# 64x64 state tiles, w_in loaded by blocks of 128 rows, and a new order in a fused attention and MLP kernel

## The chip, the cores and the metric

The kernel runs on one core of a Trainium2 chip. The metric is the device time of one execution in microseconds, median of several runs. A run more than 1.5% above the fastest of its kernel counts as slow, and only fast runs enter a ratio. A time is the median of all runs of a kernel; the difference between two kernels is that of the means of their fast runs. The core's parts are called as in the profile: PE is TensorE, DVE is VectorE, ACT is ScalarE, POOL is GpSimd, SP is SyncE.

## The reference

Linear attention with decay (4 batches, 8 heads, 768 positions, 64 channels), then a two-layer MLP with ELU on the 3072 tokens. Cut to what matters:

```python
for b in range(nb):                      # blocks of positions
    intra = einsum('bhic,bhjc->bhij', qb, kb) * Dmask
    intra = einsum('bhij,bhjd->bhid', intra, vb)
    inter = einsum('bhid,bhde->bhie', qb * lam_pow, kv_state)     # the state term
    out[:, :, sl] = intra + inter
    kv_state = lam_block * kv_state + einsum('bhsd,bhse->bhde', kb_dec, vb)
...
h = x @ w_in                             # 3072 x 512 times 512 x 2048
g = where(h > 0, h, exp(min(h, 0)) - 1)
return g @ w_out                         # 2048 x 512
```

## The kernel before

A program list decides what stands where on each engine. The kernel works on groups of 128 tokens: four single ones, then pairs. For each pair TensorE makes the scores (`psS`), a burst of attention output (`psO`) and state update (`psU`), eight first-layer blocks (`psH`) and seven second-layer blocks (`psM`, in a scheme of seven products with sums `fp`, `fd`, `fe` of the activations `gg` and sums `wf` of w_out). The parts that the argument touches:

```python
def emit_wi(i):                          # 8 loads, 256 columns each, on GpSimd's queue
    nc.gpsimd.dma_start(out=wi16[i][:],
        in_=moe_w_in[:, f0 : f0 + WI[i] * 128].rearrange("(k p) f -> p k f", p=128))

def att_P(g):                            # attention output of one group
    for hp in range(NHP):                # 4 pairs of heads
        for hh, r in enumerate(R):       # scores times v: tiles of 128x64
            nc.tensor.matmul(po[r, hp, :], lhsT=vt[:, 2*hp+hh, :], rhs=Pt[(g, hh)][:, hp, :], ...)
        if cb > 0:
            for r in R:                  # state term: 128x64, half of the rows are zeros
                nc.tensor.matmul(po[r, hp, :], lhsT=st[b][cb % 2][:, hp, r], rhs=qt[:, hp, :], ...)
...
SHARED = {8: 'D', 10: 'ED', ...}         # which sums GpSimd takes; the others are DVE's
AT = {'L': -19, 'l': 1, 'W': -13, 'T': -5, 'S': -7, 'B': -5}   # places in the steady part
...
if w == "S":
    ...
    late.pop(0)(); late.pop(0)()         # two maskings of scores go to DVE at once
```

## Time and profile before

| | before |
|---|---|
| time, median | 212.53 us (212.11 to 212.75); medians of 212.6 to 213.3 in later rounds |
| TensorE busy | 195.4 of 210.7 us |
| first second-layer block | 20.87 us |
| first burst of a pair (its state update) | 49.17 us |
| first of the seven-product blocks | 97.48 us |
| steady period, one pair | 15.50 us |

The three moments cut the run into stages: the start (to 49 us), the middle (to 97 us, first pairs and weight sums) and the rest. They are read from TensorE's timeline.

### The profile page before, as it was taken

The page shows a single profiled execution, that of the slowest core. Times are in us where ns is not written, and L with a number is a line of the kernel's source. Part 1 is how long each engine was busy: PE and PEld are TensorE (multiplying, and loading weights), DVE is VectorE, ACT ScalarE, POOL GpSimd, SP SyncE. Part 2 cuts the span into 40 slices and gives each one's busy share as a digit, 9 for nine tenths or more (in the row PEclk, how much of TensorE's full clock was granted, in tenths as well). Part 3 has the DMA queues.
Part 4 walks back from the last instruction along what each step waited for, and adds up shares of the span by engine and source line. Part 5 has one row for each costly group of instructions (what it writes and reads, how often), then busy time and mean ns, then how long its engine had stood idle before and what let it go on. Part 6 is the DMA issues. An engine that isn't in the chain of part 4 may idle for free.

```text
span 210.7 us, 5654 instructions
## 1 busy us (share of the span) xinstructions
PE 195.4 (93%) x2224; PEld 156.4 (74%) x2224; DVE 159.0 (75%) x294; ACT 138.0 (65%) x277; POOL 159.9 (76%) x187
## 2 busy tenths in 40 slices
PE   0687999999999999999999999999999999999993
PEld 0366776767676776767887887887988888888882
DVE  3774572689956878889979879879989889886632
ACT  4537664874877675867966967867567667667640
POOL 7999799999999999497999999996370301205961
PEclk9999999999999999999999999999999999999999
DMA  7999999999993030999949969979999911011032
GB/s 86 133 165 193 194 195 186 164 184 188 135 179 83 3 100 4 133 165 150 129 88 153 120 99 153 116 93 154 153 79 180 106 51 52 3 50 50 3 121 78
DMA packets 102122, 24.61 MB, mean 117 GB/s; under 512 B 92624, under 2 KB 99280, under 8 KB 102096
## 3 DMA queue, kind: packets, MB, share of 16 engines
q0 software_dynamic: 79760, 13.50, 83.5%
q1 hardware_dynamic: 22336, 10.76, 27.1%
q8 instruction: 17, 0.28, 0.5%
q14 instruction: 9, 0.07, 0.2%
HBM read 27.27 MB, written 6.29 MB: 159 GB/s over the span
## 4 chain that ended last, share of the span: by engine, by line
PE 66%; DVE 9%; POOL 8%; ACT 7%; DMA 4%; issue 3%; ACTq 0%; POOLq 0%; DVEq 0%
PE psH L700 30%; PE psM L567 18%; PE psM L725 11%; DMA wo<-in_moe_w_out_dram 4%; ACT e L706 3%; ACT psH L707 3%; DVE gg L666 3%; PE psS L305 3%; PE psO L341 2%; DVE g L666 2%; PE psO L347 1%; POOL wi L150 1%; POOL fe L498 1%; POOL vn L108 1%; POOL kn L108 1%
## 5 line engine op out<-in xcount | busy, mean ns | idle before, releaser
L700 PE MATMUL psH<-xt,wi 128*128 128x256 f16 (+1 forms) x896 | 99.6, 258 | 2.9 <-DVE gg L666 1.3
L700 PEld LDWEIGHTS <-wi 128*128 128x128 f16 x896 | 77.8, 98 | 17.8 <-issue 4.3
L706 ACT ACTIVATE e<-psH 128x512 f32<-128x512 f32 x96 | 57.3, 597 | 47.0 <-PE psH L700 46.0
L707 ACT ACTIVATE psH<-psH 128x512 f32<-128x512 f32 x96 | 57.0, 593 | 0.0
L666 DVE SCALAR_TENSOR_TENSOR gg<-e,psH 128x512 f16<-128x512 f32 x64 | 43.7, 682 | 15.8 <-ACT psH L707 15.5
L666 DVE SCALAR_TENSOR_TENSOR g<-e,psH 128x512 f16<-128x512 f32 x32 | 21.9, 684 | 17.7 <-ACT psH L707 17.5
L321 DVE TENSOR_TENSOR pp<-psS,mask 128x512 f16<-128x512 f32 x48 | 31.4, 683 | 4.0 <-PE psS L305 4.0
L725 PE MATMUL psM<-wo,g 128*128 128x512 f16 x128 | 32.1, 379 | 0.4 <-DMA wo<-in_moe_w_out_dram 0.3
L498 POOL TENSOR_TENSOR fd<-gg 128x512 f16<-128x512 f16 x20 | 24.3, 1215 | 0.1
L177 POOL TENSOR_TENSOR kd<-kn,ks 128x512 f16<-128x512 f16 x20 | 21.1, 1057 | 4.2 <-DMA kn<-in_k_dram 4.1
L518 POOL TENSOR_TENSOR wf<-wo 128x256 f16<-128x256 f16 (+1 forms) x28 | 21.1, 789 | 0.2
L498 POOL TENSOR_TENSOR fe<-gg 128x256 f16<-128x256 f16 x16 | 11.7, 729 | 12.2 <-DVE gg L666 12.1
L620 POOL TENSOR_TENSOR t<-m,m 128x256 f32<-128x256 f32 x8 | 5.9, 734 | 18.1 <-ACT m L553 18.1
L725 PEld LDWEIGHTS <-g 128*128 128x128 f16 x128 | 11.7, 98 | 10.3 <-issue 0.8
L567 PE MATMUL psM<-wf,gg 128*128 128x256 f16 x128 | 16.7, 273 | 0.1
L567 PE MATMUL psM<-wo,fp 128*128 128x256 f16 x128 | 16.5, 273 | 0.0
L567 PE MATMUL psM<-wf,fd 128*128 128x256 f16 x128 | 16.4, 273 | 0.0
L108 POOL DMA_DIRECT2D qn<-in_q_dram x13 | 14.7, 1135 | 0.9 <-POOLq L874 0.8
L108 POOL DMA_DIRECT2D kn<-in_k_dram x14 | 15.4, 1098 | 0.0
L108 POOL DMA_DIRECT2D vn<-in_v_dram x14 | 15.3, 1099 | 0.0
L501 DVE TENSOR_TENSOR fp<-gg 128x512 f16<-128x512 f16 x32 | 14.6, 455 | 0.6
L567 PEld LDWEIGHTS <-gg 128*128 128x128 f16 x128 | 11.9, 98 | 2.3 <-DVE gg L666 0.4
(62 smaller groups left out, 249.4 us busy)
## 6 DMA issues: line engine op xcount, KB each, us to landing
out_dram<-osb SPq DMA_DIRECT2D x22, 256.0 KB, 2.7
kn<-in_k_dram POOLq DMA_DIRECT2D x10, 256.0 KB, 6.5
qn<-in_q_dram POOLq DMA_DIRECT2D x10, 256.0 KB, 6.3
vn<-in_v_dram POOLq DMA_DIRECT2D x10, 256.0 KB, 8.3
wi<-in_moe_w_in_dram POOLq DMA_DIRECT2D x8, 256.0 KB, 7.5
wo<-in_moe_w_out_dram POOLq DMA_DIRECT2D x8, 256.0 KB, 8.9
kn<-in_k_dram POOLq DMA_DIRECT2D x4, 128.0 KB, 4.5
vn<-in_v_dram POOLq DMA_DIRECT2D x4, 128.0 KB, 5.7
```

The costliest lines, as they stand in the source:

```text
L108: nc.gpsimd.dma_start(out=t[:].rearrange("p b h d -> p (b h) d"), in_=src)
L177: nc.gpsimd.tensor_tensor(out=kd[:], in0=of(kg, g), in1=ks[:].unsqueeze(2).broadcast_to([128, H, 64]), op=ALU.mult,)
L321: nc.vector.tensor_tensor(out=P[:], in0=pts[hh][:], in1=mask[:, hh::2, :], op=ALU.mult)
L498: nc.gpsimd.tensor_tensor(out=out[:], in0=in0, in1=in1, op=op)
L501: lambda out=out, in0=in0, in1=in1, op=op: nc.vector.tensor_tensor(out=out[:], in0=in0, in1=in1, op=op)
L518: eng.tensor_tensor(out=out, in0=in0, in1=in1, op=op)
L567: nc.tensor.matmul(place_of(m), lhsT=lhs, rhs=rhs, start=(s == 0 and m in (3, 4, 1, 7)), stop=(s == NFT // 2 - 1), skip_group_check=True,)
L666: nc.vector.scalar_tensor_tensor(out=g.rearrange("p f c t -> p (f c t)"), in0=e[:], scalar=-1.0, in1=r[:], op0=ALU.add, op1=ALU.min,)
L700: nc.tensor.matmul(pH[:, f * n * 128 : (f + 1) * n * 128], lhsT=wi16[i][:, kk, w * 128 : (w + 1) * 128], rhs=xg[g0][:, kk, :], start=(kk = ...
L706: nc.scalar.activation(e[:], pH[:], AF.Exp)
L707: nc.scalar.activation(pH[:], pH[:], AF.Relu)
L725: nc.tensor.matmul(psM[g][:, cols], lhsT=gts[(g, j * FB + f)], rhs=wo16[i][:, w, cols], start=first and f == 0, stop=end and f == FB - 1, ...
```

## The change

It means to put the state term on 64x64 tiles, four at once, without the zero blocks. That needs another pairing of heads in the blocks of the attention output, heads j and j+4 together, so w_in's rows must come in that pairing: a tile of 128 partitions takes 64 rows from the upper half of w_in and 64 from the lower. The rest is a new program order, sums of GpSimd held behind DVE's, and other banks. The loads of groups 12 and 13 (`L12`) stood behind the transposing transfers of group 10 (`W10`) and now stand ahead of them. The core of the diff:

```diff
-    WI = [2] * 8
+    WI = [4] * 4
-        "q1 k0 iota k2 k1 q2 v0 v1 i0 i1 v2 i3 i2 o0 o1 d0 k3 q3 ...
+        "k0 k1 k2 iota q1 q2 v0 v1 i0 i1 i2 i3 v2 i6 i7 i4 i5 d0 o0 o1 q3 k3 ...
-        "... T0 T1 S0 S1 T2 P0 P1 S2 1:0:0 U0 1:1:0 P2 ... W10 L12"
+        "T0 S0 T1 T2 S1 P0 U0 S2 P1 1:0:0 1:1:0 P2 ... 1:6:3 L12 B:P8:P9:U8:U9 ... G6 W10"
+    SPOP = 1                                    # one masking at once, not two
-    COMB = nc.gpsimd
+    COMB = nc.vector
-    SHARED = {8: 'D', 10: 'ED', 12: 'ED', ...}
-    AT = {'L': -19, 'l': 1, 'W': -13, 'T': -5, 'S': -7, 'B': -5}
+    SHARED = {8: 'E', 10: 'PE', 12: 'ED', ...}
+    AT = {'L': -19, 'l': 2, 'W': -14, 'T': -10, 'S': -8, 'B': -5}
 ...
+        i, kk = divmod(i, NHP)
+        rows = moe_w_in.rearrange("(hf k p) f -> k hf p f", hf=2, p=64)
         nc.gpsimd.dma_start(
-            out=wi16[i][:], in_=moe_w_in[:, f0 : ...].rearrange("(k p) f -> p k f", p=128),
+            out=wi16[i][:, kk, :], in_=rows[kk, :, :, f0 : f0 + WI[i] * 128]
         )
 ...
+    for a in range(2):                          # state term, four tiles at once
+        for i in range(2):
+            for c in range(2):
+                for e in range(2):
+                    nc.tensor.matmul(po[e][R[c], a, i, :],
+                        lhsT=st[(g + i) % B][cb % 2][R[e], 2 * c + a, :],
+                        rhs=qkT[g + i][0][R[e], 2 * c + a, :], ...)
 ...
+    if own and shared:                          # GpSimd reads DVE's last sum first
+        nc.gpsimd.tensor_copy(seen_by[:], ap)
```

In the program list `T`, `S`, `P`, `U` are transposes, scores, attention output and state update of a group, `1:` and `2:` blocks of the two layers, `B:` a burst, `i`, `o`, `q`, `k`, `v` loads, `d` the decayed k on GpSimd, `F` and `G` sums of w_out on DVE and on GpSimd, `L12` the loads of groups 12 and 13, `W` the transposing transfers and the decayed k of a later group.

## The prediction

> **What bounds the kernel now.** I read the page's busy times first, then the timeline of TensorE, and only then the other engines.
>
> ```profile
> span 210.7 us, 5654 instructions
> PE 195.4 (93%) x2224; PEld 156.4 (74%) x2224; DVE 159.0 (75%) x294; ACT 138.0 (65%) x277; POOL 159.9 (76%) x187
> PE   0687999999999999999999999999999999999993
> ```
>
> TensorE is the bound from about 21 us to 207 us. Its idle time sits almost wholly in the first four slices and the last. A busy PE is not a PE at its peak, however, so I measured start to start in its timeline. Eight matmuls of 256 columns go by in 0.87 us when nothing hinders them (109.34 to 110.21 below). One period of the steady part, two groups of 128 tokens, is 15.50 us: in the chain of waits the first block after the scores starts at 97.55, 113.05, 128.55, 144.05. It holds 15 such blocks, 13.1 us. What is the rest? This is the end of one period, TensorE and then VectorE:
>
> ```profile
> 109.34 1.04 PE L567 MATMUL psM<-wf,fd 128*128 128x256 f16 x8
> 110.21 1.04 PE L700 MATMUL psH<-xt,wi 128*128 128x256 f16 x8
> 111.46 1.03 PE L700 MATMUL psH<-xt,wi 128*128 128x256 f16 x8 [0.21 <-DVE gg L666]
> 112.42 0.62 PE L305 MATMUL psS<-qT,kT 64*128 64x128 f16 x16
> 112.98 0.39 PE L567 MATMUL psM<-wf,gg 128*128 128x256 f16 x2
> ```
> ```profile
> 110.72 0.69 DVE L666 SCALAR_TENSOR_TENSOR gg<-e,psH 128x512 f16<-128x512 f32 x1 [0.70 <-ACT psH L707]
> ```
>
> Two first-layer blocks stand back to back. There are two psH banks, and the second block waits until gg has emptied the bank filled two blocks earlier: 110.21 to 111.46 is 1.25 us in place of 0.87, so 0.38 us are lost. From 111.46 to the scores at 112.42 is 0.96, so 0.09 us go where the tile shape changes. The scores take 0.56. The burst of attention output and state takes the rest:
>
> ```profile
> 132.07 0.25 PE L341 MATMUL psO<-pp,vn 128*64 128x128 f16 x2
> 132.16 0.22 PE L347 MATMUL psO<-qT,st 128*64 128x128 f16 x2
> ...
> 132.99 0.42 PE L418 MATMUL psU<-vn,kd 128*64 128x64 f16 x16
> 133.34 1.05 PE L567 MATMUL psM<-wo,fp 128*128 128x256 f16 x8
> ```
>
> From 132.07 to 132.99 pass 16 score-times-v and 16 state matmuls, 28.8 ns each; the 16 state updates take 0.35 us, 21.9 ns each. With 0.09 of change before it, the burst is 1.37. Sum: 13.1 + 0.38 + 0.09 + 0.56 + 1.37 = 15.5, as measured.
>
> The start is bound by something else. GpSimd issues all loads in order, and the second layer's first weights land late:
>
> ```profile
> 11.70 1.49 POOL L158 DMA_DIRECT2D wo<-in_moe_w_out_dram  x2
> 13.12 1.15 POOL L177 TENSOR_TENSOR kd<-kn,ks 128x512 f16<-128x512 f16 x1
> ```
> ```profile
> 18.61 1.96 PE L700 MATMUL psH<-xt,wi 128*128 128x128 f16 x32 [0.91 <-DMA wi<-in_moe_w_in_dram]
> 20.87 1.27 PE L725 MATMUL psM<-wo,g 128*128 128x512 f16 x4 [0.30 <-DMA wo<-in_moe_w_out_dram]
> ```
>
> **What the Trainium skill says.** "TensorE: Matmul & The Clock Gate", Part 3, says that matmuls on different tiles of the array run at once, and that a weight load overlaps running matmuls only where the row group differs. The trace agrees with the first: 28.8 ns for 128 columns on half-array tiles, against 55.6 ns for 128 columns on the whole array (16 in 0.89 us). "TensorEngine Tiling (Array Packing)", Tiling Modes, says that changing the mode drains TensorE; that is the 0.09 us above. "SBUF — State Buffer", Who interferes with whom, says that a VectorE instruction with two SBUF inputs contends with a GpSimd instruction that reads SBUF, by an exclusive lock. The trace fits: the sum fp on VectorE takes 0.42 us alone and 0.58 to 0.59 while GpSimd sums, and GpSimd's fd 1.15 or 1.34. "DMA: Bandwidth & Descriptors", Anatomy of one DMA, says that many descriptors can be emitted before their incremental cost shows. The trace agrees: GpSimd takes 0.75 us to issue a w_out load of 256 rows, 0.78 for w_in's 512, 0.89 for 1,024, 1.17 for 2,048.
>
> **The change, part by part.**
>
> *State term.* Still 160 matmuls of 128 columns, now 64x64, four tiles at once. Before: 16 per burst at 28.8 = 0.46 us. Full fourfold overlap gives 0.23; the 21.9 ns that the state updates need, though they stream only 64 columns, suggest a floor of load and issue, and 0.35. The 64x64 part also has to change to the 128x64 tiles of the scores, another 0.09. So 0.32 to 0.44 in place of 0.46: 0.02 to 0.14 per burst, ten bursts, 0.2 to 1.4 us. I take 0.4.
>
> *Order.* The scores now stand between the two first-layer blocks. Their 0.56 us (with 0.09 of drain) fill the wait of 0.38. From a block's end to its free bank I read 0.26 + 1.09 (exp and relu) + 0.03 + 0.69 (gg) + 0.05 = 2.12 us. The old order gave the bank two blocks, 1.75; the new gives 1.75 + 0.65 = 2.40. Six such places stand between 94.7 and 172 us in the trace, five of 0.38 and one of 0.24: 2.1 us. The one at 188 us has no scores left and stays.
>
> *VectorE in the steady part.* Removed: half of the state update (one of 128 partitions in place of two of 64, 0.68 each), and in most periods a sum. Added: the combinations u and t, now read from PSUM (0.41 each). By the listing of the new order, a period such as that of group 10 has 8 gg, 4 pp, 2 xt, 1 st, 4 fd, and 5 short ones: 15 x 0.61 + 4 x 0.4 + 5 x 0.34 = 12.5 us (distances start to start) against about 13.1 busy before. No new bound. Going through a period by hand, every gg ends 0.15 us or more before its bank is wanted.
>
> *GpSimd in the steady part.* It loses u and t (2 x 0.73) and gains fp in place of fd and small copies that hold it behind VectorE; where it takes all three sums (group 16) it has 4 x 3.1 + 0.7 + three loads 3.5 = 16.6 us of work in a 15.1 us period. Those sums are wanted 6 us or more after they can start, so this delays nothing. Old states: 16 quarter products of 0.64 (10.2 us) become 2 whole ones; ScalarE takes 24 short scalings (0.35 start to start) in place of 16.
>
> *Zeroing.* Four 0.27 us memsets of VectorE and four 0.40 us of ScalarE go; none is on the path.
>
> *Start.* The set of loads ahead of the first w_out is the same, but w_in's first 1,024 columns are eight issues and not four. At an estimated 0.72 each (the trend of the issue times above), eight take 5.8 us where four took 3.1. So kd0, which stood at 13.1 to 14.3, ends at about 15.7, and the new order puts the first state update U0, which needs it, ahead of scores 2, output 1 and every first-layer block; TensorE works in order and stands until then. The first-layer start moves from 14.4 to about 17.0, and the first second-layer block from 20.9 to about 22.0. The larger packets give some back: in the trace's packet records, 512-byte packets pass at 350 per us, 1,024-byte ones at 195, so all of w_in takes 10.5 us of DMA and not 11.7. With fewer small waits afterwards I expect 0.6 us left as a loss at 35 us.
>
> *35 to 97 us.* The old kernel loses about 1.9 us to waits here (back-to-back blocks at 62, 77 to 80, 94, and the scores at 55). Moved scores and the lighter state update should take back some 0.7.
>
> *Tail.* TensorE is dense until its last matmul at 207.3 and stays so. Nothing.
>
> Sum: -0.4 - 2.1 - 0.7 + 0.6 = -2.6 us, 209.9. I put 209.7.
>
> **The rivals.** (a) The start costs more: if each w_in issue takes 0.8 us or a kd waits, loads stay late to 50 us and the start loses 2 us; then 211.5. For it: GpSimd is busy 5.0 of every 5 us there. (b) The start costs nothing, because it waits for the same weights either way, the 64x64 tiles overlap fully, and 35 to 97 us gains 1.5 us: -1.4 - 2.1 - 1.5 = 207.5. For it: the order was chosen anew as a whole. Against: the issue count. (c) ScalarE's four scalings now come one block earlier, ahead of the exp of the block before the burst; if they delay that gg past its bank's use, or VectorE's five short operations do, 0.2 to 0.4 us per period come back and the order's gain is gone: 211.5 to 212. Against: the blocks around the burst leave 0.9 us.
>
> **Range and chances.** Central 209.7; the rivals span 207.5 to 212, so 207.0 to 212.2. Two per cent is 208.3, which needs rival (b) nearly whole: 0.27. Slower by 2% would need a fresh stall of 6 us: 0.03.
>
> **What would show it.** Right: periods of 15.0 to 15.1 us in the steady part, no wait for gg at the second first-layer block, state matmuls at 22 ns or less each with a gap of 0.09 after them, and a first-layer start near 17 us after a wait for kd. Wrong: periods still near 15.4 with new waits for gg or pp; a start before 15.5 us; GpSimd's sums named as what TensorE waits for.

## More of the kernel before

The prediction shows how the steady part is read. One part of the page that it did not show turned out to matter, the count of DMA packets (packets, megabytes, and how many lie under a size; then GpSimd's queue, q0, with packets, MB and share of the engines' time):

```profile
DMA packets 102122, 24.61 MB, mean 117 GB/s; under 512 B 92624, under 2 KB 99280, under 8 KB 102096
q0 software_dynamic: 79760, 13.50, 83.5%
```

## The result, and the profile after

The changed kernel took 226.43 us (median of four, 225.0 to 230.5, the highest a slow run), the kernel before 212.64 in the same rounds. The ratio is 1.063 (95% interval 1.055 to 1.071). A ratio is the mean time of one kernel's fast runs over that of the other's of the same rounds, so it is not quite the ratio of the medians. The prediction was 209.7 us with a range to 212.2; the result lies far outside, and on the other side.

The profile taken with this result fell into a slow run, so the lines below are from a fast run of the same kernel on another occasion (run e1 below, 224.26 us). First the page, the lines that answer to those of before:

```profile
span 222.5 us, 5672 instructions
PE 195.1 (88%) x2224; PEld 155.1 (70%) x2224; DVE 150.3 (68%) x280; ACT 137.7 (62%) x285; POOL 166.4 (75%) x213
PE   0536796869999999399999999999999999999993
DMA packets 114538, 24.67 MB, mean 111 GB/s; under 512 B 107088, under 2 KB 111696, under 8 KB 114512
q0 software_dynamic: 92176, 13.56, 84.8%
```

TensorE has as much to do as before (195.1 us), and it stands idle for 27.4 us in place of 15.3. The row of tenths shows where: slices 2 to 9, and one slice with a 3 in the middle. The bytes are the same, yet there are 12,416 more packets on q0, and the packets under 512 bytes rise by 14,464.

The steady part is what was predicted. TensorE's timeline of one period (start, us, engine, line, operation, tile):

```profile
124.09 1.04 PE L750 MATMUL psH<-xt,wi 128*128 128x256 f16 x8
125.06 0.62 PE L319 MATMUL psS<-qT,kT 64*128 64x128 f16 x16
125.61 1.05 PE L750 MATMUL psH<-xt,wi 128*128 128x256 f16 x8
...
130.08 0.42 PE L387 MATMUL psO<-qT,st 64*64 64x128 f16 x16
130.43 0.64 PE L357 MATMUL psO<-pp,vn 128*64 128x128 f16 x16
130.90 0.42 PE L458 MATMUL psU<-vn,kd 128*64 128x64 f16 x16
```

The scores stand between two first-layer blocks and nothing waits. The 16 state matmuls take 0.35 us start to start, 21.9 ns each (before 28.8). Period: 15.03 us (119.72 to 134.75 for the same block).

The start is where the time went. POOL and PE, in order of time:

```profile
12.08 2.45 POOL L158 DMA_DIRECT2D wi<-in_moe_w_in_dram  x3
16.97 0.79 POOL L158 DMA_DIRECT2D wi<-in_moe_w_in_dram  x1 [2.44 <-DMA wi<-in_moe_w_in_dram]
17.77 1.06 POOL L184 TENSOR_TENSOR kd<-kn,ks 128x512 f16<-128x512 f16 x1
18.89 0.61 PE L449 MATMUL psU<-vn,kd 128*128 128x128 f16 x4 [5.46 <-POOL kd L184]
...
20.54 3.59 PE L750 MATMUL psH<-xt,wi 128*128 128x128 f16 x32
...
27.86 0.59 PE L775 MATMUL psM<-wo,g 128*128 128x512 f16 x2
```

GpSimd stands 2.44 us before it can issue a piece of w_in, because an earlier piece has not landed. The waits fit a limit of eight loads under way, taken in turn, so that the ninth waits for the first: counted back from 16.97, the eighth load before is the first piece of w_in, issued at 8.04, and w_in's pieces land 8.2 to 10.6 us after issue. The same count fits the load at 22.69 here and the one at 14.33 in e4 below. Behind that load stands the decayed k of group 0, behind it the state update U0, and TensorE works in order: it waits 5.46 us. Its first 32 first-layer matmuls then take 3.59 us, some 110 ns each. That is not the loads' doing: in e2 below, whose loads are mended, the same 32 take 3.59 us too. No run here tests what slows them; the granted clock is 1.00 there. Before, the first 16 took 1.58 and the next 16 took 1.06. The first second-layer block comes at 27.86 us, 7 us later than before.

In the middle stands the other stop. Loads of group 12 on POOL, transposing transfers of group 10 on SP's queue, and TensorE:

```profile
84.77 1.20 POOL L111 DMA_DIRECT2D qn<-in_q_dram  x1
85.97 1.15 POOL L111 DMA_DIRECT2D kn<-in_k_dram  x1
86.36 1.29 SPq L285 DMA_TRANSPOSE kT<-kn  x1
87.10 1.16 POOL L111 DMA_DIRECT2D vn<-in_v_dram  x1
...
94.20 0.62 PE L319 MATMUL psS<-qT,kT 64*128 64x128 f16 x16 [3.32 <-DMA kT<-kn]
```

The transposing transfer issued at 86.36 set free the scores only at 94.2, nearly 8 us later. For the transposing transfers between 60 and 104 us the view of this source line says:

```profile
DMA to landing us min/median/max: 2.5/4.0/8.4
```

So this transfer was among the slowest, while three loads of 256 KB issued in the same 3.5 us were under way. Before, the same transfers of group 10 were issued long ahead of the loads of group 12, and the scores of groups 10 and 11 did not wait:

```profile
73.48 1.22 SPq L271 DMA_TRANSPOSE qT<-qn  x1
74.75 1.26 SPq L271 DMA_TRANSPOSE kT<-kn  x1
81.34 0.62 PE L305 MATMUL psS<-qT,kT 64*128 64x128 f16 x16
82.05 1.21 POOL L108 DMA_DIRECT2D qn<-in_q_dram  x1
```

Counted from the first burst, these transposes did not move (24.3 us after it before, 24.1 now), but the loads did, from 32.9 to 23.8 us. The change's own order brought the two together, not the late start.

Cut into the three stages (from the timelines of fast profiled runs; the "rest" runs to the end):

| kernel | first burst at | middle | rest | span |
|---|---|---|---|---|
| before | 49.17 | 48.30 | 113.27 | 210.7 |
| after (e1) | 60.97 | 50.50 | 111.02 | 222.5 |

The rest gained 2.25 us. The start lost 11.8 and the middle 2.2.

### The profile page after: what moved, and what is told of

Same layout as the page of the kernel before. It is cut to its first block, busy times and chain, and to the rows that moved or that the text cites. A ratio compares the mean times of both kernels' runs of the same rounds, so it can differ in the third digit from the quotient of the medians.

```text
span 228.7 us, 5672 instructions
## 1 busy us (share of the span) xinstructions
PE 199.7 (87%) x2224; PEld 158.0 (69%) x2224; DVE 150.9 (66%) x280; ACT 137.9 (60%) x285; POOL 166.5 (73%) x213
## 2 busy tenths in 40 slices
DMA packets 114538, 24.67 MB, mean 108 GB/s; under 512 B 107088, under 2 KB 111696, under 8 KB 114512
## 4 chain that ended last, share of the span: by engine, by line
PE 70%; DMA 16%; POOL 8%; DVE 2%; ACT 1%; issue 1%; POOLq 0%; SPq 0%; ACTq 0%
PE psH L750 32%; PE psM L617 20%; PE psM L775 10%; DMA wi<-in_moe_w_in_dram 9%; DMA kn<-in_k_dram 4%; DMA kT<-kn 4%; PE psS L319 3%; PE psO L357 2%; PE psO L387 2%; POOL wi L158 1%; POOL wo L165 1%; POOL kn L111 1%; POOL vn L111 1%; POOL qn L111 1%; POOL kd L184 1%
## 5 line engine op out<-in xcount | busy, mean ns | idle before, releaser
L750 PE MATMUL psH<-xt,wi 128*128 128x256 f16 (+1 forms) x896 | 103.3, 265 | 5.4 <-DMA wi<-in_moe_w_in_dram 4.1
L750 PEld LDWEIGHTS <-wi 128*128 128x128 f16 x896 | 79.7, 102 | 21.9 <-DMA wi<-in_moe_w_in_dram 5.4
L716 DVE SCALAR_TENSOR_TENSOR g<-e,psH 128x512 f16<-128x512 f32 x32 | 21.9, 685 | 27.9 <-ACT psH L757 23.0
L335 DVE TENSOR_TENSOR pp<-psS,mask 128x512 f16<-128x512 f32 x48 | 32.1, 683 | 6.3 <-PE psS L319 6.2
L775 PE MATMUL psM<-wo,g 128*128 128x512 f16 x128 | 34.8, 401 | 0.5 <-DMA wo<-in_moe_w_out_dram 0.5
L550 POOL COPY tc<-fd 128x1 f16<-128x1 f16 x16 | 3.0, 188 | 30.6 <-DVE fd L543 30.6
L184 POOL TENSOR_TENSOR kd<-kn,ks 128x512 f16<-128x512 f16 x20 | 20.9, 1047 | 0.3 <-DMA kn<-in_k_dram 0.3
L775 PEld LDWEIGHTS <-g 128*128 128x128 f16 x128 | 12.2, 102 | 10.8 <-issue 2.6
L552 POOL TENSOR_TENSOR fe<-gg 128x256 f16<-128x256 f16 x28 | 18.7, 667 | 0.0
L552 POOL TENSOR_TENSOR fd<-gg 128x512 f16<-128x512 f16 x16 | 18.4, 1153 | 0.0
L158 POOL DMA_DIRECT2D wi<-in_moe_w_in_dram x16 | 12.9, 834 | 4.1 <-DMA wi<-in_moe_w_in_dram 4.1
L111 POOL DMA_DIRECT2D vn<-in_v_dram x14 | 15.7, 1119 | 0.0
L552 POOL TENSOR_TENSOR fp<-gg 128x512 f16<-128x512 f16 x12 | 13.9, 1156 | 0.4 <-DVE gg L716 0.2
```

What stands on the lines that cost most here:

```text
L111: nc.gpsimd.dma_start(out=t[:].rearrange("p b h d -> p (b h) d"), in_=x[b : b + n, :, c * L : (c + 1) * L].rearrange("b h p d -> p (b h) d"),)
L158: nc.gpsimd.dma_start(out=wi16[i][:, kk, :], in_=rows[kk, :, :, f0 : f0 + WI[i] * 128])
L184: nc.gpsimd.tensor_tensor(out=kd[:], in0=of(kg, g), in1=ks[:].unsqueeze(2).broadcast_to([128, H, 64]), op=ALU.mult,)
L335: nc.vector.tensor_tensor(out=P[:], in0=pts[hh][:], in1=mask[:, hh::2, :], op=ALU.mult)
L552: nc.gpsimd.tensor_tensor(out=out[:], in0=in0, in1=in1, op=op)
L716: nc.vector.scalar_tensor_tensor(out=g.rearrange("p f c t -> p (f c t)"), in0=e[:], scalar=-1.0, in1=r[:], op0=ALU.add, op1=ALU.min,)
```

## The experiments

Theory A: pieces of w_in whose source has two halves of 64 rows are moved by few DMA engines, and this holds up the start. The Trainium skill says on "DMA: Bandwidth & Descriptors", in "Why a DMA increments its semaphore by 16 and not by 1", that the number of engines is found from the slowest dimension of each access pattern, and that the generator "picks the largest k ≤ 16 that divides both of those dim sizes". The tile's side has 128 partitions; the source's slowest dimension is the two halves. So k would be 2 instead of 16. The count of packets agrees: on q0 the records hold 15,376 packets of 4 bytes against 912 before. The additional 14,464 are 16 for each of eight more transfers, and 14,336, which is 16 transfers times 14 engines times 64. The packets' start times agree too: from 12 to 16 us, e1 starts 346 packets of 1,024 bytes on q0 and has at most 12 under way at once; e4, with as many pieces but each in one part, starts 489 and has up to 23. One packet takes 98 ns in both. Another reading is left open: the 4-byte packets themselves take time, 151 us summed over the engines in e1 against 16 in e4. No run parts the two, and the experiments below test the form of the loads as a whole. Rivals: it is the number of transfers, the new order, or the collision in the middle. Twelve kernels were run.

**e1_after_again.** The changed kernel as it is, to compare within the same rounds.

> The changed kernel again, for a profile of the fast state and an interval. Theory A (the w_in transfers): each of the 16 w_in transfers has a source in two pieces of 64 rows (outer size 2), so only two of the sixteen DMA engines carry its data; the trace shows 1,024-byte packets passing at only some 80 to 100 per us while w_in loads (195 per us for w_out in the kernel before), and 14,336 extra packets of 4 bytes = 16 transfers x 14 engines x 64. Then the start is again about 9 us late at the first second-layer block (29.7 against 20.9 us) and about 12 us late when the last block of w_in is used (46.9 against 35.0). The stall of 5 us for a transposed kT at 93 us in the slow profile is either chance (then it is gone here: span near 223.5) or part of it (still there).

Measured: 227.15 us (224.26 to 229.8, the highest a slow run), ratio 1.072 (1.065 to 1.078). The result repeats, and the stop for kT is there again; its fast profile is the one above. The first second-layer block is 7.0 us late, not 9.

**e2_halves.** The same layout in the tile, loaded in eight transfers of 64 partitions with four blocks of rows each. The result stays correct.

```diff
-        nc.gpsimd.dma_start(out=wi16[i][:, kk, :], in_=rows[kk, :, :, f0 : ...])
+        hf, odd = divmod(kk, 2)
+        if not odd:
+            nc.gpsimd.dma_start(out=wi16[i][hf * 64 : hf * 64 + 64],
+                in_=moe_w_in[hf * 256 : hf * 256 + 256, f0 : ...].rearrange("(k p) f -> p k f", p=64))
```

> The changed kernel with one thing undone: w_in comes in 8 transfers of 64 partitions by four row blocks (256 rows, outer size 64 on both sides), the same bytes into the same tiles at the same places of the order. Theory A (two engines per transfer): the packets of 4 bytes fall from 15,376 to about 1,000, w_in lands as fast as w_out, the start is at or within 1 us of the kernel before, and with the steady periods of 15.03 us the time is 208 to 211 us. Rival B (the new order of the start, U0 waiting for kd0 ahead of the first layer, costs the time): the first second-layer block stays near 27 us or later and the time stays above 218. Rival C (the state term, GpSimd's sums): no change, 225.

Measured: 219.01 us (217.97 to 220.76), ratio 1.030 (1.025 to 1.035), 7.0 us below e1. The packets under 512 bytes are back at 92,624. The first second-layer block comes at 22.86 us, the first burst at 53.41. So the form of the loads alone costs 7 us, but 6 remain: the start is 2.0 us late and the time far above theory A's 208 to 211, and of rival B's signs only the time is there. The stop in the middle is still there, and now with a second part (TensorE's timeline):

```profile
86.28 1.03 PE L322 MATMUL psS<-qT,kT 64*128 64x128 f16 x16 [3.15 <-DMA kT<-kn]
87.25 1.89 PE L778 MATMUL psM<-wo,g 128*128 128x512 f16 x4
88.93 1.91 PE L753 MATMUL psH<-xt,wi 128*128 128x256 f16 x8
```

Blocks of 1.03 and 1.04 us take 1.89 and 1.91: the granted clock was 0.50 from 85 to 90 us. The stop costs 3.15 us and the low clock some 2.5 more. "TensorE: Matmul & The Clock Gate", section "Why this matters for your kernels", advises against idle gaps of TensorE above some 3 us between bursts, because the clock falls back to half. This agrees here, though not always: the stop of 3.32 us in e1 was followed by blocks of 1.04.

**e3_before_twopiece.** The other direction: the kernel before with sixteen two-piece loads and nothing else. Its result is wrong, since the rows no longer match.

```diff
-    WI = [2] * 8
+    WI = [4] * 4
+        rows = moe_w_in.rearrange("(hf k p) f -> k hf p f", hf=2, p=64)
+        for kk in (2 * half, 2 * half + 1):
+            nc.gpsimd.dma_start(out=wi16[i][:, kk, :], in_=rows[kk, :, :, cols])
```

> The kernel before with only its w_in loads replaced: 16 transfers of 128 rows each in two pieces of 64 rows, as the change has them (the result is wrong on purpose, since the rows then do not match the heads). Theory A: the start is late as in the changed kernel, 8 to 14 us lost, time 220 to 227. Rival B: the order of before keeps it at 212 to 215, the issues costing at most 3 us.

Measured: 229.2 us (227.28 to 231.28, the highest a slow run), ratio 1.074 (1.069 to 1.079), above theory A's 220 to 227. The loads alone bring the whole loss into the old order: first second-layer block at 29.41, first burst at 62.29, and the same 107,088 packets under 512 bytes.

**e4_before_blocks.** The same with sixteen loads of 128 consecutive rows, so the number of transfers without the two pieces.

```diff
+        rows = moe_w_in.rearrange("(k p) f -> k p f", p=128)
+        for kk in (2 * half, 2 * half + 1):
+            nc.gpsimd.dma_start(out=wi16[i][:, kk, :], in_=rows[kk, :, cols])
```

> The kernel before with its w_in loads as 16 transfers of 128 consecutive rows (one piece, outer size 128), the result right. It has the count of issues and the packet size of the change without the two pieces. Theory A: 0 to 3 us lost, by eight more issues of about 0.75 us on GpSimd; no packets of 4 bytes beyond those of the semaphores. A rival that blames the number of transfers or GpSimd's issue time: as late as the run with two pieces, 220 or more.

Measured: 217.58 us (216.17 to 217.64), ratio 1.021 (1.017 to 1.024). More than theory A allowed. The table of stages shows where: the first burst is only 1.6 us late (50.76), the middle loses 1.8 (a stop of 2.00 us for kT), the rest 1.6 (blocks of 1.74 and 1.91 us behind the stop). This stop is another one than that of e1: here the scores of group 13 wait, because GpSimd comes to the loads of group 12 at 85.63 (before 82.05) and the transposes of groups 12 and 13, which need them, follow 3.5 us later than before. So sixteen transfers are a small loss, and a start that shifts a little is enough to set off a stop in the middle, also in the old order. The two pieces cost 11.3 us on top (e3 against e4).

**e5_halves_oldstart.** e2 with the start order of the kernel before (loads, U0 behind the first first-layer block), the order of the change from 46 us on.

```diff
-        "k0 k1 k2 iota q1 q2 v0 v1 i0 i1 i2 i3 v2 ...
+        "q1 k0 iota k2 k1 q2 v0 v1 i0 i1 i2 i3 v2 i6 i7 i4 i5 o0 o1 d0 k3 q3 ...
-        "T0 S0 T1 T2 S1 P0 U0 S2 P1 1:0:0 1:1:0 ...
+        "T0 T1 S0 S1 T2 P0 P1 S2 1:0:0 U0 1:1:0 ...
```

> The kernel after with its first-layer weights in eight transfers of 64 partitions (as in e2) and with the start order of the kernel before (same order of loads on GpSimd's queue, head-state products after the first first-layer block, iota second); from 46 us on the order of the kernel after. Theory A (the two-piece loads and the new start order each cost; the steady part gains): the first first-layer block comes at about 14.5 us and the first second-layer block at about 21 us, the first use of the last weight block at about 35 us and the first burst at 48 to 49 us; the stall before the scores of groups 12 and 13 stays (2 to 4 us and the half clock after it), so 212 to 215 us. Rival B (the new order of the start is harmless and only the loads cost): no gain over e2, 218 to 220 us.

Measured: 218.09 us, ratio 1.022 (1.020 to 1.025), three fast runs from 217.07 to 218.09 and two slow ones, 230.08 and 230.94. The profiled run is slow, so its lengths are not compared: in it TensorE stood 17.6 us at 55 us. Neither theory had that; e6 shows a shorter stop there in a fast run. The time is rival B's and not theory A's, though the fast runs are 1.7 us below e2's.

**e6_halves_oldstart_l12.** e5 with the loads of group 12 placed ahead of most w_out sums on GpSimd (issued from 58.5 us on).

```diff
-  ... T7 2:3:1 G2 1:4:3 S6:7 G3 ... 1:6:3 L12 B:P8:P9:U8:U9 ...
+  ... T7 Lq12 Lk12 2:3:1 G2 1:4:3 S6:7 Lv12 G3 ... 1:6:3 B:P8:P9:U8:U9 ...
```

> As e5, with the loads of groups 12 and 13 issued earlier (ahead of GpSimd's second half of weight sums). Theory A: the stall before the scores of groups 12 and 13 and the low clock after it are gone, so 4 us less than e5: 208 to 211 us, what had been predicted for the change. Rival B (the stall comes from something other than the late loads, such as the transposing transfers themselves): same as e5.

Measured: 213.81 us (212.44 to 214.73 and one slow run of 217.87), ratio 1.002 (0.997 to 1.007), 4.1 us below e5, as theory A said, though above its range. The scores of group 10 wait no more. What stayed is this, POOL, DVE and PE:

```profile
50.23 6.17 POOL L572 TENSOR_TENSOR wf<-wo 128x256 f16<-128x256 f16 x8
50.90 5.79 DVE L572 TENSOR_TENSOR wf<-wo 128x256 f16<-128x256 f16 x4
...
58.66 1.89 PE L752 MATMUL psH<-xt,wi 128*128 128x256 f16 x8 [3.05 <-DVE g L718]
```

Four w_out sums on DVE take 5.79 us beside eight of GpSimd. In e4, where GpSimd made no such sums meanwhile, the same four took 1.08. DVE's queue is behind them, TensorE waits 3.05 us for g, and the clock falls again (0.50 from 58.6 to 61 us). That GpSimd's sums hold up DVE's fits the exclusive lock that the prediction cited, with DVE shut out for several instructions of GpSimd in a row. It matters who comes first: here GpSimd began 0.67 us ahead, in e1, e2 and e7 DVE began 0.1 to 0.4 us ahead, and the four sums took 2.46 to 2.70 us.

**e7_halves_newstart_l12.** e2 with the early loads of group 12, so with the start order of the change.

> As e2 (eight transfers, new start order), with the loads of groups 12 and 13 issued earlier. Theory A: the stall of 3 us and the half clock behind it go, so 4 us less than e2: 214 to 216 us; the start stays 4 us late. Rival B (the clock drop belongs to the late start): no change from e2, 219 us.

Measured: 214.07 us (213.37 to 215.58), ratio 1.006 (1.002 to 1.010), 4.9 us below e2. Theory A holds. The clock is full throughout. One wait for kT of 1.57 us remains at 71 us, where the moved loads now meet the transposes of groups 8 and 9.

**e8_before_order.** The kernel before with the scores and transposes of the steady part one place earlier, nothing else.

```diff
-    AT = {..., 'T': -5, 'S': -7, 'B': -5}
+    AT = {..., 'T': -6, 'S': -8, 'B': -5}
```

> The kernel before with one thing of the change: scores and transposes of the steady part one place earlier, so that the scores lie between the two first-layer blocks. Theory A: the wait of the second of two adjacent first-layer blocks goes (0.38 us a period), so the steady period is 15.1 instead of 15.5 us and the time 210.5 to 211.3 us. Rival B: the period only shifts the wait to another block, and the time stays 212.5 us.

Measured: 215.48 us (215.12 to 215.99), ratio 1.012 (1.010 to 1.014). Theory A failed: the period is 15.70 us, longer than 15.50. Rival B is right that the wait only moves, but the time rose as well. TensorE and DVE in one period:

```profile
129.30 1.05 PE L700 MATMUL psH<-xt,wi 128*128 128x256 f16 x8
129.68 1.28 DVE L321 TENSOR_TENSOR pp<-psS,mask 128x512 f16<-128x512 f32 x2
130.88 0.67 DVE L666 SCALAR_TENSOR_TENSOR gg<-e,psH 128x512 f16<-128x512 f32 x1
131.61 1.05 PE L700 MATMUL psH<-xt,wi 128*128 128x256 f16 x8 [0.39 <-DVE gg L666]
```

The two maskings now come just ahead of gg on DVE, and the wait of 0.39 us has moved to the next first-layer block.

**e9_repaired.** e6 with the DVE sums of w_out moved to the end of GpSimd's, and two maskings at once in the first four groups.

```diff
-  ... 2:3:2 U3 F4 2:3:0 ... G6 W10
+  ... 2:3:2 U3 2:3:0 ... G6 W10 G4
-            for _ in range(SPOP):
+            for _ in range(2 if a[0] < 4 else SPOP):
```

> As e6 (eight transfers, start order of before, loads of groups 12 and 13 early), with the one set of w_out sums that lay on DVE moved to the end of GpSimd's sums, so that no DVE sum of this kind runs beside GpSimd's, and with both maskings of the scores at once in the first four groups as before. Theory A (in e5 and e6 the DVE sums were starved by GpSimd's and PE stood still 3 to 18 us at 55 us): that stop goes and the clock stays up, so 4 us less than e6's profile: 207.5 to 209.5 us, faster than before by 1.5 to 2.5 per cent, and no run far above the others. Rival B (the stop has another cause): 213 us, as e6.

Measured: 210.58 us (209.77 to 211.34), no slow run, ratio 0.989 (0.986 to 0.992), 1.1% faster than before: clear of noise. Theory A holds in kind: the stop at 55 us is gone, the clock is full. Its range was 1 us too low. What the two maskings add was not tested by itself.

**e10_repaired_256.** e9 with w_in in sixteen transfers of 64 partitions and 256 columns.

```diff
-    WI = [4] * 4
+    WI = [2] * 8
```

> As e9, with w_in in sixteen transfers of 64 partitions and 256 columns (the packet size of before) instead of eight of 512 columns. Theory A (each transfer has a cost of its own: issue on GpSimd and one of eight places under way): the first second-layer block comes 0.5 to 1.5 us later than in e9, time 0.5 to 2 us above it. Rival B (the larger packets are what made the start slower than before): the start is that of before, 20.9 us, time 0.5 to 1 us below e9.

Measured: 209.88 us (208.75 to 210.14), ratio 0.985 (0.981 to 0.988). The intervals of e9 and e10 overlap, so it is at most a little faster; theory A's 0.5 to 2 us of loss are not there. Rival B is not shown either: the first second-layer block comes at 22.30 us (22.09 in e9), not at 20.9. This is the fastest kernel, faster than both.

**e11_repaired_oldsums.** e9 with the sums as before: shared out as there, not held behind each other, combinations on GpSimd.

```diff
-    COMB = nc.vector
+    COMB = nc.gpsimd
-    SHARED = {8: 'E', 10: 'PE', 12: 'ED', 14: 'PE', ...}
+    SHARED = {8: 'D', 10: 'ED', 12: 'ED', 14: 'ED', ...}
```

> As e9, with the sums of the steady part as in the kernel before: shared out between DVE and GpSimd as there, GpSimd's not held behind DVE's, and the combining sums on GpSimd. Theory A (the sums beside each other cost DVE time, which the order of the change cannot bear): DVE's sums fe and fp take 470 and 450 ns or more instead of 283 and 420 ns, waits of first-layer blocks for gg come back, the steady period is 15.3 to 15.6 instead of 15.03 us and the time 2 to 4 us above e9. Rival B (this part only moves work off the critical path): period 15.03 to 15.1 us, same time as e9.

Measured: 212.53 us (211.94 to 213.0), ratio 0.998 (0.995 to 1.002), 1.9 us above e9. From its groups of instructions (busy us, mean ns | idle before them):

```profile
L545 DVE TENSOR_TENSOR fp<-gg 128x512 f16<-128x512 f16 x32 | 16.1, 502 | 0.6
L545 DVE TENSOR_TENSOR fe<-gg 128x256 f16<-128x256 f16 x16 | 8.1, 504 | 0.0
```

In e9 they take 420 and 282 ns. The time is just under theory A's 2 to 4 us, and waits for gg come back (1.5 us in all after 60 us). The period is rival B's: most are 15.03 us. In the profiled runs 0.6 of the 2.4 us lie before the first burst, where the two programs do the same, so they are not the sums'. The rest sits in the middle (0.8) and behind it (0.9): the first four second-layer blocks there take 9.06 us (99.26 to 108.32) against 8.26 in e9.

**e12_before_order_one.** e8 with one masking at once from group 8 on.

```diff
-            late.pop(0)()
-            late.pop(0)()
+            for _ in range(2 if a[0] < 8 else 1):
+                late.pop(0)()
```

> As e8 (the kernel before with the scores one place earlier), but with one masking of the scores instead of two put ahead of the next gg on DVE, as the change does. Theory A (in e8 the second masking delayed gg, and the wait of 0.38 us moved to the block after): the period falls from 15.70 us to 15.1 to 15.3 us and the time to 210.5 to 212 us. Rival B (the old sums on DVE and GpSimd are what hold gg up): the period stays 15.5 to 15.7 us, 213 to 215 us.

Measured: 212.95 us (211.91 to 216.88, the highest a slow run), ratio 0.999 (0.994 to 1.003), 2.9 us below e8. The period is 15.13 us, so theory A is right on its main point. The rest of the run gains 1.26 us on before (112.01 against 113.27); the middle gives 1.1 back, with a wait of 1.35 us for kT at about 97 us (the scores of group 13, which now come earlier; e8 has the same wait), so the total stays.

The stages of all fast profiles, in us:

| kernel | first burst at | middle | rest | span |
|---|---|---|---|---|
| before | 49.17 | 48.30 | 113.27 | 210.7 |
| after (e1) | 60.97 | 50.50 | 111.02 | 222.5 |
| e2: loads mended | 53.41 | 52.67 | 111.01 | 217.1 |
| e3: before, two-piece loads | 62.29 | 49.59 | 113.63 | 225.5 |
| e4: before, 16 loads | 50.76 | 50.10 | 114.91 | 215.8 |
| e6: e2, old start, early loads | 50.71 | 51.21 | 111.01 | 212.9 |
| e7: e2, early loads | 52.14 | 48.44 | 111.02 | 211.6 |
| e8: before, scores earlier | 49.97 | 49.39 | 114.61 | 214.0 |
| e9: e6, no DVE sums beside | 51.25 | 46.53 | 111.02 | 208.8 |
| e10: e9, 256 columns | 50.72 | 46.52 | 111.01 | 208.3 |
| e11: e9, old sums | 51.89 | 47.37 | 111.94 | 211.2 |
| e12: e8, one masking | 49.24 | 49.39 | 112.01 | 210.6 |

## Why the prediction was wrong

**The step that failed is "Start".** It reads: "With fewer small waits afterwards I expect 0.6 us left as a loss at 35 us." The loss is 11.8 us at the first burst. Two terms of it were wrong, and one wait was missing.

- "The larger packets give some back: [...] all of w_in takes 10.5 us of DMA and not 11.7." This looked at the size of a packet and not at how the transfer is spread over the engines. The experiments show that the two-piece form alone makes 7.0 us in the new order (e1 against e2), and 11.3 in the old (e3 against e4). That only two engines carry the data of such a transfer follows from the skill's rule and fits the packet counts and times; it is not shown, as which engine moved which packet is not in the trace.
- "At an estimated 0.72 each": the issues took 0.82 us (median), so rival (a)'s 0.8 was right. This too comes with the two pieces: pieces of the same size in one part took 0.58 (e4). But rival (a) expected 2 us from it, and the issues are the lesser part.
- The wait of 2.44 us for a place among eight loads under way was in no sum; rival (a) had "a kd waits", but not for this reason nor of this size. U0 waits for kd0 as predicted, but kd0 ends at 18.8 us and not 15.7; the first first-layer block starts at 20.54 and not 17.0, and the first second-layer block at 27.86 and not 22.0.

**"35 to 97 us" failed too.** It put down a gain of 0.7 us; the middle lost 2.2 in e1 and 4.4 in e2. The lighter work is there: without stops the middle takes 46.53 us (e9), a gain of 1.8. What was missed is that the new order issues the loads of group 12 together with the transposing transfers of group 10, whose scores then wait (3.32 us in e1, 3.15 in e2, with half a clock behind the second). e7 and e6 show that moving these loads removes this stop. The transposes of other groups have little slack as well: the scores of group 13 wait 1.35 to 2.00 us in e3, e4, e8 and e12, and those of group 8 wait 1.57 in e7.

**State term, right in kind, its size too small.** 21.9 ns each against "22 ns or less"; the burst of 1.27 us became 1.17, so 0.10 us each, in the upper part of "0.02 to 0.14". Over ten bursts that is 1.0 us where the sum had 0.4.

**Order, right, and a little too large.** The two first-layer blocks with the scores took 2.77 us before (125.71 to 128.48) and take 2.41 (124.09 to 126.50): 0.36 us a period. Both together make 15.50 into 15.03, as "periods of 15.0 to 15.1 us" said. The reason given was incomplete: e8 shows that the order alone only moves the wait. It needs one masking at a time as well (e12, 15.13 us), and this the prediction did not name.

**DVE and GpSimd in the steady part, right.** Nothing new binds there. The part was put down as "this delays nothing"; e11 shows that the new sums are worth 1.9 us at most, as DVE's sums are no longer slowed.

**Zeroing** was not tested by itself, and **Tail** lost about 0.3 us in the seven-product blocks of the last pair (2.06 us for one that took 1.75 before), for which no run was spent.

**The rivals.** None came near, as only (a) made the start cost more, and by 2 us. e9 and e10, which keep the state term, the sums and the steady order, and undo the loads, the start order, the place of the loads of group 12 and the sums of w_out on DVE, run at 210.58 and 209.88 us against the predicted 209.7. That they come so near is partly luck: in e9 the start loses 2.1 us where the sum had 0.6, the middle gains 1.8 where it had 0.7, and the rest gains 2.25 where it had 2.5. From the change to e9: the form of the loads 7.0 us, the loads of group 12 4.9, the start order with the moved w_out sums 3.7. The last step changes three things at once, and its shares are only read from the stages of two profiled runs, 2.8 us apart: 0.9 us before the first burst, 1.9 in the middle, of which 1.57 is the stop in e7.

## What to carry to other kernels

When a change alters how a load is cut, read its access pattern from the slowest dimension and not from the packet size: one that begins with a dimension of two can take the whole transfer down, and the count of tiny packets on the page tells it at once. Before trusting a gain in the steady part, look for the transfers and sums elsewhere that just fit: loads moved some blocks ahead collided with transposes, sums of two engines shut each other out, and some of these stops brought a lower clock. An order that removes a wait must be followed through the engine behind it, as the wait may simply move.

## What the Trainium skill lacked or had wrong

- "DMA: Bandwidth & Descriptors", the number of engines: the rule agrees with what was seen. The page does not say how such a transfer looks in a profile: 896 packets of 4 bytes for each of these transfers beyond the usual 16 (14,336 for sixteen transfers), at most 12 packets of 1,024 bytes under way at once against 23, and a cost of 11.3 us in a run with sixteen of them (e3 against e4).
- None of the pages looked at has a transposing transfer behind plain loads: landing 8.4 us after issue at most, 4.0 in the median and 2.5 at least, in the 44 us around three loads of 256 KB.
- "SBUF — State Buffer", Who interferes with whom: the lock agrees, but a single instruction's length is not the whole wait. Four sums of DVE that take 1.08 us without GpSimd's took 5.79 beside eight of GpSimd's in a row that began ahead of them (e6), and TensorE stood for 3.05 us behind them. Where DVE began first, the four took 2.46 to 2.70 (e1, e2, e7).
- "TensorE: Matmul & The Clock Gate": gaps of 3.15 us (e2) and 3.05 (e6) were followed by half the clock, as the page's 3 us has it. So was one of 2.00 (e4, granted clock 0.50 from 102.4 to 104 us), below the page's figure; one of 3.32 (e1) was not. 3 us is no sharp limit here.
